# A build-time ordered attention kernel: a longer planned DMA landing, queries projected directly for the first head group, and transposes for the last four units

## The chip, the cores and the metric

The kernel runs on one core of one Trainium2 chip. The metric is the device time of one execution in microseconds (us). Every kernel was run several times; the text gives medians and the single times where they matter. A profile is of one execution. Engines are abbreviated as in the profile: PE is the matmul engine (PEld its weight loads), ACT the scalar engine, DVE the vector engine, POOL the general-purpose engine, and SP the engine that issues nearly all DMAs (SPq in the profile).

## The reference, cut to what matters

Two attention blocks are computed from their own inputs and concatenated. Block A is softmax attention over 2048 positions with 32 heads of 20 elements; block B is linear attention. Both project inputs to queries, keys and values first and project their outputs last. All inputs are bf16.

```python
# A: B, S, D, H = 1, 2048, 640, 32 ; Dh = 20
q, k, v = split(x @ wqkv)
scores = einsum("bhqd,bhkd->bhqk", q, k) * (Dh ** -0.5)
p = softmax(scores)
a = einsum("bhqk,bhkd->bhqd", p, v).reshape(B, S, D) @ wo
# B: phi(t) = where(t > 0, t + 1, exp(t)) + 1e-6 ; no softmax, num / den
...
return concatenate([a, b], axis=-1)          # (1, 2048, 1280)
```

Most of the work is in block A: 32 heads times 2048 x 2048 scores have to be exponentiated.

## The kernel before

The kernel does not leave order to the moment of execution. While it is built, a list scheduler (`_Plan`) simulates the engines with assumed durations and assumed latencies, and so fixes the order of instructions in each engine's list. On the chip each engine works through its list and waits on semaphores where data is not there. The assumed latencies therefore set no wait and no time; they only decide how much other work stands between a DMA and the instruction that uses what it brings.

```python
_LAT = {"pe": 0.16, "act": 0.12, "dve": 0.12, "pool": 0.14, "sp": 2.8, "none": 0.0}   # us

class _Plan:
    ...
    def run(self, t, s0):                    # t is the task chosen, s0 its planned start
        ...
        t.end = s0 + dur
        ...
        for k in t.kids:                     # who depends on t
            k.t0 = max(k.t0, t.end + _lat(e, k.eng))
    ...

    def spd(self, fns, deps, reads, writes, prio=2.0):      # a group of DMAs on SP
        def fn(t):
            self.sch.dma_group("sp", fns, reads=reads, writes=writes)
        return self.plan.add(_Task("sp", 0.62 * len(fns), fn, prio=prio), deps)
```

So `"sp": 2.8` says: what a DMA brings can be used 2.8 us after its issue.

Block A is cut into 8 groups of four heads and 4 columns of 512 queries: 32 "units" n, each planned to take 24.5 us. In a unit PE computes scores into banks `ps`, ACT exponentiates most of them (`f_PT<-ps`, 667 instructions in all), DVE does the rest by a polynomial (`f_Y`, `f_T`), and PE multiplies the results with the values. At the end of a unit DVE evacuates the sums (`f_OTr<-ps`) and the unit is normalised: the row sums go to a denser layout by a DMA, their reciprocals through DRAM and back as a broadcast by two more, and a multiply writes the result. The evacuation of unit n also waits for the multiply of unit n-2, because the buffer `OTr` has two halves.

```python
    def t_norm(self, n, ev):                 # ev: the evacuation of unit n
        ...
        prev = self.mult[n - 1] if n else None
        if n in self.quick:
            a = self.dve(0.62, tr1, (ev, prev), prio=0.2)    # DVE transpose  Rbc <- OTr
            a = self.dve(0.25, rc1, (a,), prio=0.2)          # reciprocal     Rc  <- Rbc
            last = self.dve(0.62, tr2, (a,), prio=0.2)       # DVE transpose  Rbc <- Rc
            pr = 0.2
        else:
            d1 = self.spd([lambda e: e.dma_start(Rc, OTr[0:128:32, o, :])],
                          (ev,), (("OTr", o),), (("Rc", o),))
            a = self.dve(0.25, rc, (d1,), prio=2.0)          # reciprocal, in place
            d2 = self.spd([lambda e: e.dma_start(nd, Rc)], (a, prev), (("Rc", o),), (("Nd", o),))
            last = self.spd([lambda e: e.dma_start(Rbc[:], nd.unsqueeze(1).broadcast_to([4, 32, 512]))],
                            (d2,), (("Nd", o),), ("Rbc",))
            pr = 2.0
        self.mult[n] = self.dve(0.62, mult, (last,) + outdep, prio=pr)    # OTw <- OTr * Rbc
        if n < self.NU - 1:
            self.ostore[n] = self.spd([...], (self.mult[n],), ...)        # Od <- OTw, 4 DMAs
```

`self.quick = {NU - 1}`: only the last unit uses the transposes. `t_oload` loads columns of `Od` back (`f_OTp<-f_Od`) for the output projection.

Queries and keys of later groups are projected for 128 channels at a time, copied to one of three `qkp` slots, stored to DRAM and loaded in the head layout (`t_qk`, `t_kload`, `t_qload`). Group 0 has its keys, and the queries of column 0, projected straight into the head layout with padded weights (`t_pad`); its queries of columns 1 to 3 take the trip through DRAM.

```python
        self.kq[("Q", 0)] = [self.t_pad("Q", 0, (ex[0],), 0.0, 0.1)]
        ...
        first = [("Q", 0, 1), ("K", 0, 0), ("K", 1, 0), ("Q", 0, 2), ...]      # 16 jobs of t_qk
        for k, (w, c2, tc) in enumerate(first):
            jobs.append((ut[1] - 9.0 + k * (ut[4] - ut[1] - 10.0) / len(first), w, c2, tc))
        ...
        self.t_qload(0, 1, 2)
        self.t_qload(0, 2, 4)
```

A mask for block B is made in five steps, each a POOL instruction and two DVE instructions that wait for each other. The plan books it as 3.0 us of POOL and no DVE.

```python
    def make_mask(self):
        for c in range(N_DC):                                  # 5 times
            sch.op("pool", lambda e: e.iota(it, ...))
            sch.op("dve", lambda e: e.tensor_scalar(mf, it, 0.0, None, op0=ALU.is_le), ...)
            sch.op("dve", lambda e: e.scalar_tensor_tensor(self.mask[:, c], it, -19.0, mf, ...), ...)
```

Of the kernel before, what the change touches and what calls it, by code (L numbers as in the profile page):

```python
# [718 lines left out]
def _lat(a, b):  # L719
    if a == b:  # L720
        return {"dve": 0.05, "sp": _LAT["sp"]}.get(a, 0.0)
    return _LAT[a]


_LAT = {"pe": 0.16, "act": 0.12, "dve": 0.12, "pool": 0.14, "sp": 2.8, "none": 0.0}


class _Task:
    __slots__ = ("eng", "dur", "fn", "left", "kids", "prio", "end", "t0", "acq", "rel", "bank",
                 "due", "win", "mode", "ready", "seq", "cond", "occ", "over", "work", "pace")  # L730

    def __init__(self, eng, dur, fn, prio=2.0, acq=None, rel=(), due=None, win=None, mode=None,
                 cond=None, occ=None, over=1.0, work=0.0, pace=False):
        self.eng = eng
        self.dur = dur
        self.occ = dur if occ is None else occ
        self.fn = fn
        self.left = 0
        self.kids = []
        self.prio = prio  # L740
        self.end = None
        self.t0 = 0.0
        self.acq = acq
        self.rel = rel
        self.bank = None
        self.due = due
        self.win = win
        self.mode = mode
        self.cond = cond
        self.over = over  # L750
        self.work = work
        self.pace = pace


class _Plan:
# [20 lines left out]
    def add(self, task, deps=()):  # L776
        task.seq = self.seq
        self.seq += 1
        self.open += 1
        for d in deps:  # L780
            if d is None:
                continue
            if d.end is None:
                d.kids.append(task)
                task.left += 1
            else:
                task.t0 = max(task.t0, d.end + _lat(d.eng, task.eng))
        if task.left == 0:
            self.avail[task.eng].append(task)
        return task  # L790
# [67 lines left out]
    def run(self, t, s0):  # L858
        e = t.eng
        self.now = s0  # L860
        self.avail[e].remove(t)
        if e == "pe" and self.filler is not None and s0 - self.free[e] > self.FGAP:
            self.filler(t, s0)
        if t.acq is not None:
            tok = self.banks[t.acq]
            x = min(tok)
            tok.remove(x)
            t.bank = x[1]
        dur, occ = t.dur, t.occ
        if e == "pe":  # L870
            if t.mode is not None and t.mode != self.mode:
                x = max(0.0, self.SW - (s0 - self.free[e]))
                dur += x
                occ += x
                self.mode = t.mode
            self.hist.append((s0, occ, t.work))
            if len(self.hist) > 64:
                del self.hist[:32]
        t.end = s0 + dur
        self.free[e] = s0 + occ  # L880
        self.busy[e] += occ
        extra = t.fn(t)
        if extra:
            t.end += extra
            self.free[e] += extra
        for pool, src in t.rel:
            b = src.bank if isinstance(src, _Task) else src
            self.banks[pool].append((t.end + _LAT[e], b))
        for k in t.kids:
            k.t0 = max(k.t0, t.end + _lat(e, k.eng))  # L890
            k.left -= 1
            if k.left == 0:
                self.avail[k.eng].append(k)
        self.open -= 1
# [20 lines left out]
class _Fast:  # L915
# [154 lines left out]
    def mid_consts(self):  # L1070
        sch, ps = self.sch, self.ps
# [4 lines left out]
               writes=("Vc0",))  # L1076
        sch.op("pool", lambda e: e.memset(vv[:, :, 21:22], 0.0), writes=("Vc1",))
        sch.op("pool", lambda e: e.memset(self.cst[:], 0.0), writes=tuple(("cst", g) for g in range(N_GRP)))
        sch.op("pool", lambda e: e.memset(self.Qr[:, 0, 512:], 0.0), writes=("Qz",))
        sch.op("pool", lambda e: e.memset(self.Qr[:, 1, :], 0.0), writes=("Qz",))  # L1080
        sch.op("pool", lambda e: e.memset(self.ones[:], 1.0), writes=("ones",))
        sch.op("pool", lambda e: e.memset(self.kvZ[:], 0.0), writes=("kvZ0",))
# [97 lines left out]
    def dve(self, dur, fn, deps, prio=2.0, rel=(), due=None):  # L1180
        return self.plan.add(_Task("dve", dur, fn, prio=prio, rel=rel, due=due), deps)

    def spd(self, fns, deps, reads, writes, prio=2.0):
        def fn(t):
            self.sch.dma_group("sp", fns, reads=reads, writes=writes)
        return self.plan.add(_Task("sp", 0.62 * len(fns), fn, prio=prio), deps)

    def t_pad(self, which, tc, deps, due, prio):
        sch, ps = self.sch, self.ps
# [2 lines left out]
        def mms(b):  # L1192
            for c in range(N_DC):
# [1 line left out]
                       start=(c == 0), stop=(c == N_DC - 1), reads=(("wpad", k), ("xT", c, tc)),  # L1195
                       writes=(("ps", b),), inc=(c == N_DC - 1))
                yield
        first, last = self.bg(mms, [512] * 5, deps, due, 1e9, prio=prio, over=1.0)
        self.use(("xT", tc), last)
        if which == "Q":  # L1200
            dst, res = self.Qr[:, 0, 0:512], (("Q", 0, 0),)
        else:
            dst, res = self.KT[:, 0, 512 * tc:512 * (tc + 1)], (("K", 0, tc),)

# [248 lines left out]
    def t_norm(self, n, ev):  # L1453
# [45 lines left out]
        if n < self.NU - 1:  # L1499
            self.ostore[n] = self.spd([lambda e, i=i: e.dma_start(  # L1500
                self.Od.ap()[80 * g + 20 * i:80 * g + 20 * i + 20, 512 * qc:512 * (qc + 1)],
                self.OTw[32 * i + 1:32 * i + 21, ow, :]) for i in range(4)], (self.mult[n],), (("OTw", ow),),
                (("Od", g, qc),))
        return self.mult[n]

    def t_oload(self, qc, part):
# [8 lines left out]
        else:  # L1515
            fns = [lambda e: e.dma_start(self.OTp[:, k, 0:4, :], od[0:512, col].rearrange("(c p) q -> p c q", p=128)),
                   lambda e: e.dma_start(self.OTp[0:48, k, 4, :], od[512:560, col])]
        return self.spd(fns, deps, rd, (("OTp", k),))

    def t_out(self, qc, tl, h, part, deps, due, prio=4.0):  # L1520
        sch, ps = self.sch, self.ps
# [43 lines left out]
            self.parts1[(tl, h)] = ev  # L1565
        if part != 1 and h == 1:
            d = self.spd([lambda e: e.dma_start(self.out[128 * t:128 * (t + 1), 0:D_MODEL], self.stage[:, s, :])],
                         (ev,), (("stage", s, 0), ("stage", s, 1)), (("out", t),))
            self.stg[(s, 0)] = self.stg[(s, 1)] = d
        return last  # L1570

# [330 lines left out]
    def run(self):  # L1902
# [10 lines left out]
        self.phil = {}  # L1913
        self.mult = {}
        self.outA = {}
        self.quick = {NU - 1}
        self.dkall = set(_LK[:max(self.m)])
        plan.banks["aux"] = [(0.0, 6), (0.0, 7)]
        plan.avail["dq"] = []
# [22 lines left out]
        self.ostore = {}  # L1942
        self.parts1 = {}
        self.xlast = []
        self.kq[("Q", 0)] = [self.t_pad("Q", 0, (ex[0],), 0.0, 0.1)]
        for tc in range(NQC):
            self.kq[("K", 0, tc)] = [self.t_pad("K", tc, (ex[tc],), ut[0] + tc * U / 4 - 4 if tc else 0.0,
                                                0.2 if tc == 0 else 2.2)]
        mid = _Task("pool", 1.0, lambda t: self.mid_consts())
        plan.add(mid, (self.kq[("Q", 0)][0],))  # L1950
        wol = plan.add(_Task("pool", 4.5, lambda t: self.wo_load()),
                       [self.kq[("K", 0, tc)][0] for tc in range(NQC)])
        for t in range(NT):
            self.t_v(t, 0, (ewv, ex[t // 4], mid), ut[0] + t * U / 16 - 1.5, 16.0)
        cons = {}
        jobs = []
        for t in range(NT):
            jobs.append((ut[2] + t * 5 * U / 16, "V", t, 1))
        first = [("Q", 0, 1), ("K", 0, 0), ("K", 1, 0), ("Q", 0, 2), ("K", 0, 1), ("K", 1, 1), ("Q", 0, 3),
                 ("K", 0, 2), ("K", 1, 2), ("K", 0, 3), ("K", 1, 3), ("Q", 1, 0), ("Q", 1, 1), ("Q", 1, 2),  # L1960
                 ("Q", 1, 3), ("Q", 0, 0)]
        for k, (w, c2, tc) in enumerate(first):
            jobs.append((ut[1] - 9.0 + k * (ut[4] - ut[1] - 10.0) / len(first), w, c2, tc))
        for c2, a, b in ((2, 4.5, 10.5), (3, 11.0, 15.0), (4, 16.0, 22.5)):
            for k in range(8):
                jobs.append((T0 + (a + (b - a) * k / 8.0) * U, "KQ"[k % 2], c2, k // 2))
# [13 lines left out]
        if max(self.m):  # L1980
            cons[0], cons[1] = self.t_const(0, ut[0] + 0.8 * U), self.t_const(1, ut[4])
            cons[2], cons[3] = self.t_const(2, ut[7]), self.t_const(3, ut[8])
        self.t_qload(0, 1, 2)
        self.t_qload(0, 2, 4)

        self.pvcnt = [0] * NU
        self.pvn = 0
# [254 lines left out]
```

## Time and profile before

Three runs gave 864.59, 867.81 and 875.27 us. The profile is of a further execution, of 876.45 us, slower than all (its span, first to last instruction, is 874.6 us).

| span 874.6 us | us |
|---|---|
| ACT busy | 783.9 |
| ACT waits, up to 22 us | 15.2 |
| ACT waits, 22 to 76 us (units 0 and 1) | 9.4 |
| ACT waits, after 76 us | 40.7 |
| after the last exponential (the tail) | 24.0 |

The waits in this table, and in all later ones, are the idle times of 0.15 us or more in front of ACT's instructions in its timeline, added up by the time at which they end. With ACT's busy time they make 873.2 of 874.6 us. ACT is the busiest engine, so with ACT's work as it is the kernel can only become shorter by fewer of these gaps.

The page of the kernel before: busy time by engine (share of the span, instructions), and the chain of work that ended last, by engine.

```profile
PE 761.6 (87%) x10902; PEld 260.4 (30%) x10902; DVE 688.7 (79%) x1137; ACT 783.9 (90%) x723; POOL 26.8 (3%) x52
...
ACT 54%; PE 20%; DVE 14%; DMA 9%; SPq 2%; issue 1%; POOL 0%; DVEq 0%; POOLq 0%
```

ACT is 90% busy, yet makes up only 54% of the chain that ended last; DVE and DMA have 23% of it together. Work of theirs stands in ACT's way. The view of waits says which (who waits, for what: us in total, times, longest us):

```profile
ACT f_PT L1421 <- PE ps L172: 59.1, 34, 9.4
...
DVE f_Rc L1488 <- DMA f_Rc<-f_OTr: 17.6, 6, 5.6
...
DVE f_OTw L1496 <- DMA f_Rbc<-f_Nd: 14.3, 6, 5.2
```

ACT waits for scores of PE. DVE waits twelve times, 31.9 us in all, for two of the DMAs of the normalisation. How one becomes the other is to be read from the timeline of the kernel before, from 128 to 146 us (start us, duration us, engine, line, operation, output<-input, shapes, count; in brackets the idle time before it and what ended it):

```profile
130.57 0.53 SPq L1247 DMA_DIRECT2D f_KT<-f_Kd  x1
...
131.15 1.61 SPq L1258 DMA_DIRECT2D f_Qr<-f_Qd  x4
...
132.86 0.75 DVE L1449 TENSOR_SCALAR_CACHE_REDUCE f_OTr<-ps,f_c 128x512 f32<-128x512 f32 x1 [0.30 <-PE ps L172]
...
133.64 0.56 SPq L1484 DMA_DIRECT2D f_Rc<-f_OTr  x1
...
142.13 0.25 DVE L1488 RECIPROCAL f_Rc<-f_Rc 128x16 f32<-128x16 f32 x1 [4.53 <-DMA f_Rc<-f_OTr]
...
142.30 1.16 DVE L2055 TENSOR_TENSOR f_T<-f_T,f_Y 128x2048 bf16<-128x2048 bf16 x1
...
143.51 0.40 PE L172 MATMUL ps<-f_T,f_V 128*22 128x512 bf16 x4 [4.29 <-DVE f_T L2055]
...
144.50 2.52 ACT L1421 ACTIVATE f_PT<-ps 128x1536 bf16<-128x1536 f32 x2 [4.44 <-PE ps L172]
```

The 8 KB of row sums were asked for at 133.64 us, right behind a load of 512 KB of keys and four loads of queries on the same queue. They were there at 142.1 us, 8.5 us later, where the plan had assumed 2.8. DVE stood at the reciprocal for 4.53 us. The polynomial's next step (`f_T`, 142.30) stands behind it in DVE's list, and PE needs `f_T` for a multiplication with the values: PE stood 4.29 us at 143.51. ACT's next scores come behind that matmul in PE's list, so ACT waited 4.44 us. The Trainium skill, "Perfetto Trace Analysis", in its part on the tensor engine ("Tensor Engine Instruction (MATMUL, LD_WEIGHTS)"), says that "ACT/DVE/GPSIMD are strict FIFO"; this trace agrees: in those 4.53 us DVE did nothing else, though `f_T` behind the reciprocal had had its inputs since 137.2 us.

There is a second way: at 661.04 us PE stood 5.37 us in front of scores, until DVE copied scores out to `f_Y` and so emptied a bank.

That the load in front makes the DMA late is read from two cases: of the 31 DMAs of row sums in this kernel, two stand right behind keys and four query loads, and they took 8.5 and 9.5 us from issue to use; the others took 2.8 to 6.6. DVE's longest wait, 5.64 us at 660.2 us, has another origin: the evacuation had ended at 650, but SP issued the DMA only at 655.9 us, because issuing four DMAs of block B (7.49 us) and four query loads (2.06 us) came first.

The first stage has its own gaps. ACT's timeline of the kernel before, from 15 to 75 us:

```profile
39.57 6.88 ACT L1421 ACTIVATE f_PT<-ps 128x1536 bf16<-128x1536 f32 x6 [2.08 <-PE ps L172]
...
52.58 22.71 ACT L1421 ACTIVATE f_PT<-ps 128x1536 bf16<-128x1536 f32 x20 [6.13 <-PE ps L172]
```

### The profile page before, as it was taken

The page shows a single profiled execution, that of the slowest core. Times are in us where ns is not written, and L with a number is a line of the kernel's source. Part 1 is how long each engine was busy: PE and PEld are TensorE (multiplying, and loading weights), DVE is VectorE, ACT ScalarE, POOL GpSimd, SP SyncE. Part 2 cuts the span into 40 slices and gives each one's busy share as a digit, 9 for nine tenths or more (in the row PEclk, how much of TensorE's full clock was granted, in tenths as well). Part 3 has the DMA queues.
Part 4 walks back from the last instruction along what each step waited for, and adds up shares of the span by engine and source line. Part 5 has one row for each costly group of instructions (what it writes and reads, how often), then busy time and mean ns, then how long its engine had stood idle before and what let it go on. Part 6 is the DMA issues. An engine that isn't in the chain of part 4 may idle for free.

```text
span 874.6 us, 24419 instructions
## 1 busy us (share of the span) xinstructions
PE 761.6 (87%) x10902; PEld 260.4 (30%) x10902; DVE 688.7 (79%) x1137; ACT 783.9 (90%) x723; POOL 26.8 (3%) x52
## 2 busy tenths in 40 slices
PE   6989897999999999888879888898997887988996
PEld 2423232333333332333322222232222222322332
DVE  3688686898898888888869787787786996977745
ACT  3879787999999999999979999998896997999980
POOL 3200000000000000000000000000000000000000
PEclk8999888999999999999989998999898998999998
DMA  8443112002013000130162242144032031111231
GB/s 219 146 96 89 38 39 59 24 16 57 24 48 70 24 31 23 29 90 15 45 110 62 45 123 66 45 66 129 25 102 94 26 113 50 53 47 56 74 101 64
DMA packets 82619, 57.57 MB, mean 66 GB/s; under 512 B 43628, under 2 KB 74444, under 8 KB 82508
## 3 DMA queue, kind: packets, MB, share of 16 engines
q1 hardware_dynamic: 79228, 53.29, 22.3%
q10 hardware_dynamic: 3280, 2.66, 1.0%
q8 instruction: 86, 1.41, 0.7%
q14 instruction: 25, 0.20, 0.1%
HBM read 29.63 MB, written 18.57 MB: 55 GB/s over the span
## 4 chain that ended last, share of the span: by engine, by line
ACT 54%; PE 20%; DVE 14%; DMA 9%; SPq 2%; issue 1%; POOL 0%; DVEq 0%; POOLq 0%
ACT f_PT L1421 53%; PE ps L172 20%; DVE f_Y L2041 5%; DMA f_Rc<-f_OTr 4%; DVE f_T L2050 3%; DMA f_Rbc<-f_Nd 2%; ACT f_ex L1585 2%; DVE f_T L2055 1%; DMA f_xT<-in_A_x_dram 1%; SPq L1797 1%; DMA f_Nd<-f_Rc 1%; DVE f_OTr L1449 1%; DVE f_qkp L1224 1%; DMA f_Bd<-f_dc 0%; DVE f_OTw L1496 0%
## 5 line engine op out<-in xcount | busy, mean ns | idle before, releaser
L1421 ACT ACTIVATE f_PT<-ps 128x1536 bf16<-128x1536 f32 (+1 forms) x667 | 770.1, 1309 | 60.4 <-PE ps L172 59.1
L172 PE MATMUL ps<-f_Qr,f_KT 32*128 32x512 bf16 x2048 | 307.5, 396 | 63.3 <-ACT f_PT L1421 46.5
L2041 DVE TENSOR_SCALAR f_Y<-ps 128x512 bf16<-128x512 f32 x380 | 254.7, 685 | 48.7 <-PE ps L172 45.8
L172 PEld LDWEIGHTS ps<-f_Qr,f_KT 32*128 32x128 bf16 x2048 | 75.5, 91 | 308.2 <-ACT f_PT L1421 230.4
L172 PE MATMUL ps<-f_PT,f_V 128*22 128x512 bf16 x1668 | 164.3, 394 | 0.0
L2055 DVE TENSOR_TENSOR f_T<-f_T,f_Y 128x2048 bf16<-128x2048 bf16 x95 | 115.4, 1215 | 2.0 <-PE ps L172 1.7
L2050 DVE TENSOR_TENSOR f_T<-f_Y 128x2048 bf16<-128x2048 bf16 x95 | 115.3, 1214 | 2.0 <-PE ps L172 0.6
L172 PE MATMUL ps<-f_T,f_V 128*22 128x512 bf16 x760 | 73.5, 389 | 15.5 <-DVE f_T L2050 8.6
L172 PE MATMUL ps<-f_xT,f_w 128*32 128x512 bf16 x800 | 63.1, 389 | 1.2 <-DVE f_Y L2041 0.4
L172 PE MATMUL ps<-f_wB,f_xB 128*32 128x320 bf16 x1280 | 63.0, 306 | 1.2 <-DVE f_Y L2041 0.7
L172 PEld LDWEIGHTS ps<-f_PT,f_V 128*22 128x22 bf16 x1668 | 40.8, 90 | 74.4 <-issue 68.2
L172 PE MATMUL ps<-f_Y,f_V 128*22 128x512 bf16 x380 | 38.3, 387 | 4.3 <-DVE f_OTr L1449 3.7
L172 PE MATMUL ps<-f_woB,f_pk 128*32 128x320 bf16 x640 | 33.3, 315 | 5.7 <-DVE f_Y L2041 5.1
L1581 DVE TENSOR_SCALAR f_r<-ps 128x320 f32<-128x320 f32 (+1 forms) x52 | 29.2, 561 | 10.3 <-PE ps L172 10.2
L1224 DVE CAST f_qkp<-ps 128x512 bf16<-128x512 f32 x40 | 27.4, 687 | 11.5 <-PE ps L172 11.3
L172 PE MATMUL ps<-f_w,f_xT 128*32 128x160 bf16 x1280 | 35.7, 245 | 0.6 <-DVE f_V L1283 0.2
L172 PEld LDWEIGHTS ps<-f_wB,f_xB 128*32 128x32 bf16 x1280 | 27.7, 97 | 27.7 <-issue 11.3
L172 PE MATMUL ps<-f_xB,f_wB 128*32 128x512 bf16 x400 | 33.0, 409 | 0.5 <-DVE f_Y L2041 0.3
L1496 DVE TENSOR_TENSOR f_OTw<-f_OTr,f_Rbc 128x512 bf16<-128x512 f32 x32 | 22.0, 688 | 14.4 <-DMA f_Rbc<-f_Nd 14.3
L1291 POOL TENSOR_SCALAR f_V<-f_V 128x160 bf16<-128x160 bf16 x24 | 15.8, 658 | 550.2 <-DVE f_V L1283 549.2
L172 PE MATMUL ps<-f_wo,f_OTp 128*32 128x320 bf16 (+1 forms) x616 | 30.8, 313 | 1.5 <-DVE f_xT L1554 0.5
L172 PEld LDWEIGHTS ps<-f_T,f_V 128*22 128x22 bf16 x760 | 18.8, 90 | 41.9 <-issue 15.3
(91 smaller groups left out, 416.7 us busy)
## 6 DMA issues: line engine op xcount, KB each, us to landing
f_Rbc<-f_Nd SPq DMA_DIRECT2D x31, 256.0 KB
f_Bd<-f_dc SPq DMA_DIRECT2D x16, 320.0 KB
f_wB<-f_Bd SPq DMA_DIRECT2D x20, 256.0 KB
out_dram<-f_st SPq DMA_DIRECT2D x32, 160.0 KB
f_KT<-f_Kd SPq DMA_DIRECT2D x7, 512.0 KB
f_Qd<-f_qkp SPq DMA_DIRECT2D x20, 128.0 KB
f_Kd<-f_qkp SPq DMA_DIRECT2D x20, 128.0 KB
f_Od<-f_OTw SPq DMA_DIRECT2D x124, 20.0 KB
```

The lines of the kernel that those rows point to most:

```text
L172: lambda e: e.matmul(out, lhsT, rhs, start=start, stop=stop, tile_position=tp, skip_group_check=sgc),
L1224: sch.op("dve", lambda e: e.tensor_copy(self.qkp[:, s, :], ps[:, first.bank, :]), reads=(("ps", first.bank),), writes=(("qkp", s),))
L1291: sch.op("pool", lambda e: e.tensor_scalar(vt[:, rs, li, :, 1:21], self.V[:, rs, t, :, 1:21], f, None, op0=ALU.mult), reads=(("V", t, rs), ...
L1421: sch.op("act", lambda e: e.activation(self.PT[:, s0:s0 + n, :], ps[:, b0:b0 + n, :], AF.Exp, scale=scale), reads=tuple(("ps", b0 + k) for ...
L1449: sch.op("dve", lambda e: e.tensor_scalar(self.OTr[:, o, :], ps[:, self.PVB, :], cs, 0.0, op0=ALU.add, op1=ALU.max, accum_out=self.mx[:, n ...
L1496: sch.op("dve", lambda e: e.tensor_tensor(self.OTw[:, ow, :], self.OTr[:, o, :], Rbc[:], op=ALU.mult), reads=("Rbc", ("OTr", o)), writes=( ...
L1581: sch.op("dve", lambda e: e.tensor_scalar(r1, ps[:, first.bank, 0:n], 0.0, 1e-6, op0=ALU.max, op1=ALU.add), reads=(("ps", first.bank),), w ...
L1585: sch.op("act", lambda e: e.activation(ex, ps[:, first.bank, 0:n], AF.Exp), reads=(("ps", first.bank),), writes=(("ex", k),))
L1797: m2 = self.spd([lambda e, j=j: e.dma_start(bd[:, j], self.dc[j:128:4, :].unsqueeze(1).broadcast_to([32, D_HEAD, 128])) for j in range(4)] ...
L2041: sch.op("dve", lambda e: e.tensor_scalar(self.Y[:, sl, :], ps[:, d.bank, :], float(D_HEAD) ** -0.5, None, op0=ALU.mult), reads=(("ps", d. ...
L2050: sch.op("dve", lambda e: e.tensor_tensor(self.T2[:, q2:q2 + 4, :], y, y, op=ALU.mult), reads=tuple(("Y", q + i) for i in range(4)), write ...
L2055: sch.op("dve", lambda e: e.tensor_tensor(self.T3[:, q3:q3 + 4, :], self.T2[:, q2:q2 + 4, :], self.Y[:, q:q + 4, :], op=ALU.mult), reads=t ...
```

## The change

Its intent is threefold: plan DMAs with a landing near what the trace shows (8.0 us), so that other work fills the time; take the first group's queries off the DRAM trip; and normalise the last four units by two DVE transposes in place of three DMAs. The transposes can do this because a head's row sums lie in a block of 32 rows. The Trainium skill, "VectorE: DVE Perf Modes" ("The three transpose paths"), says that DVE transposes only blocks of 32 x 32; that is what this layout wants, and the trace has 0.71 us for one of 128 x 512 in f32.

```diff
-_LAT = {"pe": 0.16, ..., "sp": 2.8, "none": 0.0}
+_LAT = {"pe": 0.16, ..., "sp": 8.0, "none": 0.0}
@@ class _Task: a field lat=None; _Plan.add and _Plan.run:
-            k.t0 = max(k.t0, t.end + _lat(e, k.eng))
+            k.t0 = max(k.t0, t.end + (_lat(e, k.eng) if t.lat is None else t.lat))
@@ spd(..., lat=None) hands it on @@ three exceptions to the 8.0:
+   store of a unit to Od:      lat=3.5 if n in self.quick else None
+   load of Od in t_oload:      lat=4.0
+   store of the output:        lat=4.0
@@ def t_pad
-        first, last = self.bg(mms, [512] * 5, deps, due, 1e9, prio=prio, over=1.0)
+        first, last = self.bg(mms, [512] * 5, deps, due, 1e9, prio=prio, over=0.7)
-            dst, res = self.Qr[:, 0, 0:512], (("Q", 0, 0),)
+            dst, res = self.Qr[:, 0, 512 * tc:512 * (tc + 1)], (("Q", 0, tc),)
@@
-        self.quick = {NU - 1}
+        self.quick = set(range(NU - 4, NU))
@@
-        self.kq[("Q", 0)] = [self.t_pad("Q", 0, (ex[0],), 0.0, 0.1)]
+        for tc in range(NQC):
+            self.kq[("Q", tc)] = [self.t_pad("Q", tc, (ex[tc],), ut[tc] - 9.0 if tc else 0.0, 2.2 if tc else 0.1)]
@@
-        first = [("Q", 0, 1), ("K", 0, 0), ("K", 1, 0), ("Q", 0, 2), ...]
+        first = [(w, c2, tc) for c2 in range(2) for tc in range(NQC) for w in "KQ"]
-            jobs.append((ut[1] - 9.0 + k * (ut[4] - ut[1] - 10.0) / len(first), w, c2, tc))
+            jobs.append((ut[1] + k * (ut[4] - ut[1] - 32.0) / len(first), w, c2, tc))
@@
-        self.t_qload(0, 1, 2)
-        self.t_qload(0, 2, 4)
... (a memset of Qr that is no longer needed goes; one dependence is added)
```

Read from the order of the built kernels: 60 more matmuls of the padded projection and 60 more fillers on PE; six more transposes and three more casts on DVE (three reciprocals change their form, and their number stays 36); on SP three fewer of each of the three normalisation DMAs, and eight query loads less.

More of the change, by code (lines that the diff above doesn't have):

```diff
@@ L722, in _lat @@
     return _LAT[a]
-_LAT = {"pe": 0.16, "act": 0.12, "dve": 0.12, "pool": 0.14, "sp": 2.8, "none": 0.0}
+_LAT = {"pe": 0.16, "act": 0.12, "dve": 0.12, "pool": 0.14, "sp": 8.0, "none": 0.0}
 class _Task:
     __slots__ = ("eng", "dur", "fn", "left", "kids", "prio", "end", "t0", "acq", "rel", "bank",
-                 "due", "win", "mode", "ready", "seq", "cond", "occ", "over", "work", "pace")
+                 "due", "win", "mode", "ready", "seq", "cond", "occ", "over", "work", "pace", "lat")
     def __init__(self, eng, dur, fn, prio=2.0, acq=None, rel=(), due=None, win=None, mode=None,
-                 cond=None, occ=None, over=1.0, work=0.0, pace=False):
+                 cond=None, occ=None, over=1.0, work=0.0, pace=False, lat=None):
         self.eng = eng
@@ L752, in __init__ @@
         self.pace = pace
+        self.lat = lat
 class _Plan:
@@ L786, in add @@
             else:
-                task.t0 = max(task.t0, d.end + _lat(d.eng, task.eng))
+                task.t0 = max(task.t0, d.end + (_lat(d.eng, task.eng) if d.lat is None else d.lat))
         if task.left == 0:
@@ L1078, in mid_consts @@
         sch.op("pool", lambda e: e.memset(self.cst[:], 0.0), writes=tuple(("cst", g) for g in range(N_GRP)))
-        sch.op("pool", lambda e: e.memset(self.Qr[:, 0, 512:], 0.0), writes=("Qz",))
         sch.op("pool", lambda e: e.memset(self.Qr[:, 1, :], 0.0), writes=("Qz",))
@@ L1181, in dve, with spd @@
         return self.plan.add(_Task("dve", dur, fn, prio=prio, rel=rel, due=due), deps)
-    def spd(self, fns, deps, reads, writes, prio=2.0):
+    def spd(self, fns, deps, reads, writes, prio=2.0, lat=None):
         def fn(t):
             self.sch.dma_group("sp", fns, reads=reads, writes=writes)
-        return self.plan.add(_Task("sp", 0.62 * len(fns), fn, prio=prio), deps)
+        return self.plan.add(_Task("sp", 0.62 * len(fns), fn, prio=prio, lat=lat), deps)
     def t_pad(self, which, tc, deps, due, prio):
@@ L1502, in t_norm @@
                 self.OTw[32 * i + 1:32 * i + 21, ow, :]) for i in range(4)], (self.mult[n],), (("OTw", ow),),
-                (("Od", g, qc),))
+                (("Od", g, qc),), lat=3.5 if n in self.quick else None)
         return self.mult[n]
@@ L1517, in t_oload @@
                    lambda e: e.dma_start(self.OTp[0:48, k, 4, :], od[512:560, col])]
-        return self.spd(fns, deps, rd, (("OTp", k),))
+        return self.spd(fns, deps, rd, (("OTp", k),), lat=4.0)
     def t_out(self, qc, tl, h, part, deps, due, prio=4.0):
@@ L1567, in t_out @@
             d = self.spd([lambda e: e.dma_start(self.out[128 * t:128 * (t + 1), 0:D_MODEL], self.stage[:, s, :])],
-                         (ev,), (("stage", s, 0), ("stage", s, 1)), (("out", t),))
+                         (ev,), (("stage", s, 0), ("stage", s, 1)), (("out", t),), lat=4.0)
             self.stg[(s, 0)] = self.stg[(s, 1)] = d
@@ L1951, in run @@
         wol = plan.add(_Task("pool", 4.5, lambda t: self.wo_load()),
-                       [self.kq[("K", 0, tc)][0] for tc in range(NQC)])
+                       [self.kq[("K", 0, tc)][0] for tc in range(NQC)] + [self.kq[("Q", tc)][0] for tc in range(NQC)])
         for t in range(NT):
@@ L1958, in run @@
             jobs.append((ut[2] + t * 5 * U / 16, "V", t, 1))
-        first = [("Q", 0, 1), ("K", 0, 0), ("K", 1, 0), ("Q", 0, 2), ("K", 0, 1), ("K", 1, 1), ("Q", 0, 3),
-                 ("K", 0, 2), ("K", 1, 2), ("K", 0, 3), ("K", 1, 3), ("Q", 1, 0), ("Q", 1, 1), ("Q", 1, 2),
-                 ("Q", 1, 3), ("Q", 0, 0)]
+        first = [(w, c2, tc) for c2 in range(2) for tc in range(NQC) for w in "KQ"]
         for k, (w, c2, tc) in enumerate(first):
-            jobs.append((ut[1] - 9.0 + k * (ut[4] - ut[1] - 10.0) / len(first), w, c2, tc))
+            jobs.append((ut[1] + k * (ut[4] - ut[1] - 32.0) / len(first), w, c2, tc))
         for c2, a, b in ((2, 4.5, 10.5), (3, 11.0, 15.0), (4, 16.0, 22.5)):
```

## The prediction

> **What bounds it now.** In the profiled run (span 874.6 us; busy table) ACT is busy 783.9 us (90%), PE 87%, DVE 79%; 53% of the chain that ended last is the exponentials (667, mean 1309 ns). ACT idles 91 us: about 17 before the first exponential, 24 after the last (850.6), about 49 in between, waiting for score matmuls (ACT timeline).
>
> Most of those 49 us follow a late DMA. Order is fixed at build time as if a landing took 2.8 us. In the DVE timeline reciprocals and multiplies wait for f_Rc (17.6 us) and f_Rbc (14.3 us; waits view); with DVE blocked no bank is freed and ACT starves: 4.5 us at 98 to 103, 6.3 at 144 to 151, 5.2 at 448, 2.7 at 524 to 552, 5.1 at 610 to 620, 6.6 at 663, 5.2 at 730: about 36 us. From issue to use f_Rc took 8.5 us at 133.6 and 9.5 at 435.5, behind KT and Qr loads in SP's queue. The Trainium skill (DMA: Bandwidth & Descriptors, "Anatomy of one DMA") gives about 2 us fixed for one DMA; these queued ones take longer. The first group costs 8.2 us (2.1 at 39.6, 6.1 at 52.6), where the mask's POOL/DVE steps and the queries' trip through DRAM meet.
>
> **What changes**, counted in the built kernels' order with the trace's durations:
> - Between a unit's evacuation and its reciprocal stand 7 to 14 us of DVE work (before 3 to 7), to its multiply 23 to 31 (before 10 to 16). That exceeds every wait seen (longest 5.6 us). I expect 30 to 36 us of ACT waits to go.
> - Queries of group 0: 60 more matmuls (about 6 us of PE), three casts of 0.69 us; two query loads and a memset go. But the longer landing holds the three qkp slots, and after 100 score matmuls, between units 0 and 1, stand about 15 us (estimate) of other PE work without a score (before: 5 and 9). I expect an ACT wait of about 10 us there, so no gain in the first group; two smaller clumps (4 us each) cost about 3 us.
> - Transposes for units 28 to 30: 1.4 us of DVE each, three DMA trips fewer; DVE is 46% busy at 825 to 850. Six of the eight last-but-one output tiles still stand after the last evacuation (before: all eight), so the tail shortens by 1 to 3 us.
> - 60 more filler matmuls, off the path.
>
> **Sum.** 876 (profiled) - 33 (DMA waits) + 3 (first stage) - 2 (tail) = about 844; other runs of before had fewer waits (864.6 to 875.3), so the new kernel should also scatter less. Predicted **842 us**, range 830 to 857. Faster by over 2%: 0.77; within 2%: 0.21; slower: 0.02.
>
> **The profile.** Right: DVE's waits for f_Rc and f_Rbc fall from 32 us to under 6; ACT waits after 150 us fall below 8 us; granted clock nearer 1; ACT busy unchanged within 3 us; one ACT wait of 8 to 12 us at 45 to 65 us; 20 to 24 us after the last exponential. Wrong: waits for f_Rc remain (then SP's issue order is at fault, not the planned landing), or ACT waits on PE reappear without DVE waiting for a DMA.
>
> **What would make it wrong.** The clump without scores may cost more than 12 us, or little. Longer planned landings may hold auxiliary banks and starve scores elsewhere. The profiled run is the slowest of before; against 864.6 the gain is smaller. PE, at 87%, may take back what the waits gave.

## The result, and the profile after

The changed kernel took 840.06 to 841.68 us in four runs, with a median of 840.87; the kernel before took 864.59 to 875.27 in four runs, with a median of 869.53. The ratio is 0.9668, with a 95% interval of 0.9605 to 0.9731. Ratios here are the mean time of one kernel's runs over that of the other's in the same rounds, so they are not quite the ratio of the medians. The changed kernel also scatters less: 0.2% against 1.2% from lowest to highest.

| us | before | after |
|---|---|---|
| span of the profiled run | 874.6 | 839.9 |
| ACT busy | 783.9 | 780.7 |
| ACT waits up to 22 | 15.2 | 15.8 |
| ACT waits 22 to 76 | 9.4 | 14.8 |
| ACT waits after 76 | 40.7 | 6.8 |
| tail | 24.0 | 21.1 |
| DVE waits for f_Rc and f_Rbc | 31.9 | 0 |
| mean granted PE clock | 0.953 | 0.979 |

The two profiles are of the kernel before in an execution slower than its runs, and of the slowest run of the kernel after; the medians fell by 28.7 us. The span fell by 34.7 us: 33.9 of waits after 76 us, 2.9 of tail and 3.2 of ACT's busy time, less 5.4 lost in the first stage and 0.6 at the start (the missing 0.7 us are waits too short for the table).

The page of the kernel after, busy time and chain:

```profile
PE 753.0 (90%) x11022; PEld 260.8 (31%) x11022; DVE 691.2 (82%) x1146; ACT 780.7 (93%) x723; POOL 27.9 (3%) x51
...
ACT 70%; PE 20%; DVE 7%; DMA 2%; SPq 1%; issue 1%; POOL 0%; DVEq 0%; POOLq 0%
```

DVE and DMA went from 23% of the chain to 9%, and ACT rose to 70%. The waits of the kernel after no longer have a line for `f_Rc` or `f_OTw` behind a DMA; ACT's own line is halved:

```profile
ACT f_PT L1421 <- PE ps L172: 31.2, 17, 10.1
```

The same unit end in the timeline of the kernel after, 133 to 149 us:

```profile
134.19 0.53 SPq L1247 DMA_DIRECT2D f_KT<-f_Kd  x1
134.76 1.62 SPq L1258 DMA_DIRECT2D f_Qr<-f_Qd  x4
...
136.47 0.74 DVE L1449 TENSOR_SCALAR_CACHE_REDUCE f_OTr<-ps,f_c 128x512 f32<-128x512 f32 x1
...
137.25 0.57 SPq L1484 DMA_DIRECT2D f_Rc<-f_OTr  x1
...
147.81 0.24 DVE L1488 RECIPROCAL f_Rc<-f_Rc 128x16 f32<-128x16 f32 x1
```

The DMA stands behind the same two loads as before. It was not made faster; the reciprocal now stands 10.6 us behind its issue, with DVE work in between, and has no bracket: it waits for nothing.

The first stage in the timeline of the kernel after, 40 to 80 us, PE and ACT:

```profile
56.36 1.03 PE L172 MATMUL ps<-f_Qr,f_KT 32*128 32x512 bf16 x6 [4.55 <-DVE f_Y L2038]
...
57.05 1.02 ACT L1421 ACTIVATE f_PT<-ps 128x1024 bf16<-128x1024 f32 x1 [4.06 <-PE ps L172]
...
59.67 0.61 PE L172 MATMUL ps<-f_Qr,f_KT 32*128 32x512 bf16 x2
...
67.31 0.39 PE L172 MATMUL ps<-f_PT,f_V 128*22 128x512 bf16 x4
...
67.76 12.99 ACT L1421 ACTIVATE f_PT<-ps 128x1536 bf16<-128x1536 f32 x11 [9.69 <-PE ps L172]
```

Two gaps of 4.06 and 9.69 us stand where the kernel before had 2.08 and 6.13. The first has the mask in front of it: DVE's mask steps run from 51.0 to 55.7 us, each waiting for POOL and POOL for it, and PE waits 4.55 us for a bank that DVE would have emptied. The second comes where PE's list has 140 other matmuls between two scores. They took PE 9.3 us, from 60.2 to 69.4 us; the longest such stretches of before, 80 and 92 matmuls, took it 3.5 and 4.9 us of work. (The prediction and the expectations give estimates of such stretches, counted in the built order: about 15 or 14.7 us for this one. They are too long: where the trace was looked at, PE took 0.5 to 0.7 of them.) ACT was not released by a score here: its next scores had been there since 60.3 us, and it waited until the matmuls at 67.31 us had read exponentials (`f_PT`) and so freed room in that buffer, which has 20 slots in the code. What stood in ACT's way is the stretch itself, which holds up multiplications with the values as well as scores.

### The profile page after: what moved, and what is told of

It reads as the page before. It is cut to its first block, busy times and chain, and to the rows that moved or that the text cites. A ratio compares the mean times of both kernels' runs of the same rounds, so it can differ in the third digit from the quotient of the medians.

```text
span 839.9 us, 24650 instructions
## 1 busy us (share of the span) xinstructions
PE 753.0 (90%) x11022; PEld 260.8 (31%) x11022; DVE 691.2 (82%) x1146; ACT 780.7 (93%) x723; POOL 27.9 (3%) x51
## 4 chain that ended last, share of the span: by engine, by line
ACT 70%; PE 20%; DVE 7%; DMA 2%; SPq 1%; issue 1%; POOL 0%; DVEq 0%; POOLq 0%
ACT f_PT L1421 68%; PE ps L172 20%; DVE f_Y L2038 2%; ACT f_ex L1585 2%; DMA f_xT<-in_A_x_dram 1%; DVE f_T L2047 1%; SPq L1033 1%; DMA out_dram<-f_st 0%; DVE f_T L2052 0%; DVE f_OTr L1449 0%; DVE f_st L1560 0%; DVE f_qkp L1224 0%; DVE f_woB L1131 0%; DVE f_st L1557 0%; DVE f_pk L1589 0%
## 5 line engine op out<-in xcount | busy, mean ns | idle before, releaser
L172 PE MATMUL ps<-f_Qr,f_KT 32*128 32x512 bf16 x2048 | 308.8, 388 | 53.4 <-ACT f_PT L1421 40.7
L172 PEld LDWEIGHTS ps<-f_Qr,f_KT 32*128 32x128 bf16 x2048 | 77.8, 91 | 297.7 <-ACT f_PT L1421 231.6
L172 PE MATMUL ps<-f_PT,f_V 128*22 128x512 bf16 x1668 | 159.8, 385 | 0.0
L1224 DVE CAST f_qkp<-ps 128x512 bf16<-128x512 f32 x40 | 27.4, 685 | 12.0 <-PE ps L172 11.7
L1291 POOL TENSOR_SCALAR f_V<-f_V 128x160 bf16<-128x160 bf16 x24 | 18.3, 761 | 493.0 <-DVE f_V L1283 492.0
L172 PE MATMUL ps<-f_zt 128*32 128x512 bf16 x388 | 33.5, 385 | 0.0
L172 PE MATMUL ps<-f_wo,f_OTp 128*32 128x320 bf16 x616 | 30.8, 313 | 1.4 <-DVE f_Y L2038 0.5
L1585 ACT ACTIVATE f_ex<-ps 128x320 f32<-128x320 f32 (+1 forms) x52 | 30.2, 580 | 1.3 <-DVE f_r L1581 1.2
L172 PE MATMUL ps<-f_xB,f_wB 128*32 128x512 bf16 x400 | 30.9, 383 | 0.1
```

What stands on the lines that cost most here:

```text
L172: lambda e: e.matmul(out, lhsT, rhs, start=start, stop=stop, tile_position=tp, skip_group_check=sgc),
L1224: sch.op("dve", lambda e: e.tensor_copy(self.qkp[:, s, :], ps[:, first.bank, :]), reads=(("ps", first.bank),), writes=(("qkp", s),))
L1291: sch.op("pool", lambda e: e.tensor_scalar(vt[:, rs, li, :, 1:21], self.V[:, rs, t, :, 1:21], f, None, op0=ALU.mult), reads=(("V", t, rs), ...
L1585: sch.op("act", lambda e: e.activation(ex, ps[:, first.bank, 0:n], AF.Exp), reads=(("ps", first.bank),), writes=(("ex", k),))
```

## The experiments

Twelve kernels ran, on three chips, each with the kernel before in the same rounds: its medians there were 873.91 us on chip 1, 872.94 on chip 2 and 873.19 on chip 3. All results were correct. Each kernel ran four times, land12 twice. The profile is of the fastest run of norm8_only, landing_undone, land5 and norm8_mask, and of the slowest of landing_only, queries_undone and land12, so its sums are somewhat low or high there. The table has the times and, from each profile, the sums of ACT's waits and the tail as defined above.

| kernel | chip | median us (range) | ratio to before, 95% | ACT waits 22–76 | ACT waits after 76 | tail | DVE waits f_Rc / f_Rbc |
|---|---|---|---|---|---|---|---|
| norm8_only | 1 | 856.0 (850.4–858.5) | 0.980 (0.976–0.984) | 8.0 | 7.0 | 36.9 | 0.7 / 4.2 |
| norm28_rest | 1 | 886.8 (879.2–891.1) | 1.014 (1.006–1.021) | 13.6 | 49.2 | 19.1 | 13.2 / 15.8 |
| landing_only | 1 | 864.4 (860.6–866.4) | 0.987 (0.983–0.992) | 18.5 | 9.5 | 38.1 | 5.3 / 3.3 |
| landing_undone | 1 | 878.8 (873.4–883.0) | 1.007 (1.002–1.012) | 15.3 | 39.8 | 16.3 | 14.1 / 16.8 |
| norm8_quick | 2 | 840.9 (835.8–844.0) | 0.963 (0.955–0.970) | 9.2 | 12.9 | 19.3 | 2.0 / 5.4 |
| quick_one | 2 | 859.6 (856.0–861.5) | 0.984 (0.977–0.991) | 15.2 | 8.0 | 39.2 | 0.2 / 0 |
| queries_undone | 2 | 850.8 (846.8–857.1) | 0.973 (0.967–0.980) | 17.1 | 15.9 | 21.2 | 4.7 / 3.5 |
| spread | 2 | 840.2 (837.1–842.3) | 0.963 (0.956–0.969) | 6.6 | 11.9 | 21.1 | 1.3 / 0 |
| after_again | 3 | 841.6 (839.0–842.5) | 0.964 (0.959–0.969) | 13.8 | 7.2 | 20.5 | 0 / 0 |
| norm8_mask | 3 | 841.2 (840.3–841.4) | 0.964 (0.960–0.969) | 7.2 | 10.6 | 22.8 | 0 / 0 |
| land5 | 3 | 850.2 (846.9–852.1) | 0.975 (0.970–0.980) | 13.9 | 9.9 | 23.9 | 6.7 / 0.8 |
| land12 | 3 | 975.8 (973.0–978.5) | 1.118 (1.110–1.126) | 11.7 | 127.9 | 35.2 | 0 / 1.5 |

The theories. A: the gain is the longer planned landing of the normalisation's three DMAs, because DVE stood in front of them. B, its rival: the gain is the direct queries, the transposes or the landing of the other DMAs. C: the transposes carry a part of the gain that the prediction put at 1 to 3 us; D, its rival: the tail comes from something else in the order.

### norm8_only: the kernel before, with the longer landing for three DMAs alone

The `lat` field is added with no other value changed, and then:

```diff
-                          (ev,), (("OTr", o),), (("Rc", o),))
+                          (ev,), (("OTr", o),), (("Rc", o),), lat=8.0)
-            d2 = self.spd([... nd, Rc ...], (a, prev), (("Rc", o),), (("Nd", o),))
+            d2 = self.spd([... nd, Rc ...], (a, prev), (("Rc", o),), (("Nd", o),), lat=8.0)
-                            (d2,), (("Nd", o),), ("Rbc",))
+                            (d2,), (("Nd", o),), ("Rbc",), lat=8.0)
```

> The kernel before, with 8.0 us planned only for the three landings of each unit's normalisation (f_Rc, f_Nd, f_Rbc); queries, transposes, all other landings as before. Theory A (the gain is DVE no longer blocked by these late landings): DVE's waits for f_Rc and f_Rbc fall from 32 us to under 6, ACT waits after 76 us of the span from about 41 us to under 9; about 836 us (832 to 842), so as fast as the changed kernel or a little faster, because the first stage keeps its 8 us of waits instead of 14. Theory B (the gain comes from the direct queries and the transposes, or from the other landings): 862 us or more.

Measured: 856.0 us; the waits after 76 us fell from 40.7 to 7.0 us. In the waits of norm8_only:

```profile
ACT f_PT L1422 <- PE ps L172: 24.5, 11, 9.1
...
DVE f_OTw L1497 <- DMA f_Rbc<-f_Nd: 4.2, 1, 4.2
```

Twelve waits of DVE for these DMAs became two (the other is 0.7 us long). Three planned numbers, and nothing else, take away 33.7 us of ACT's waits; the changed kernel takes away 33.9. (The profile is of the fastest of the four runs, against a slow one of before. The medians fell by 17.9 us although the tail grew by 12.9, which leaves 30.8.) But the time missed the range that A expected, 832 to 842 us: the tail grew from 24.0 to 36.9 us. The mechanism of A is right, and its bill had an entry that nobody had written down. The next experiments look for it.

### norm28_rest: the changed kernel, with the short landing for the same three DMAs

```diff
-                          (ev,), (("OTr", o),), (("Rc", o),))
+                          (ev,), (("OTr", o),), (("Rc", o),), lat=2.8)
... (the same for the other two)
```

> The changed kernel, with 2.8 us planned again only for the three landings of the normalisation. Theory A: DVE's waits for f_Rc and f_Rbc return (20 us or more) and the time goes to about 868 us (858 to 876). Theory B: the time stays within 4 us of the changed kernel's 840.9.

Measured: 886.8 us, as A said and slower than its range of 858 to 876. The waits of norm28_rest have both lines again:

```profile
DVE f_OTw L1496 <- DMA f_Rbc<-f_Nd: 15.8, 9, 4.1
...
DVE f_Rc L1488 <- DMA f_Rc<-f_OTr: 13.2, 3, 4.9
```

29.0 us of DVE's waits came back, and ACT's waits after 76 us rose to 49.2 us. So these three DMAs are necessary for the gain as well as sufficient for its main term; the 8.0 of all other DMAs, the direct queries and the transposes together do not replace them. Why this kernel is slower than landing_undone, which has 2.8 everywhere, is not settled; ACT also waits 8.0 us for DVE in block B here (`f_ex`), and the runs scatter by 12 us.

### landing_only: the kernel before, with the change's landing and nothing else

```diff
-_LAT = {..., "sp": 2.8, ...}
+_LAT = {..., "sp": 8.0, ...}
+   lat=4.0 for the load of Od and the store of the output
```

> The kernel before with the longer landing for all DMAs (4.0 for output loads and stores), without direct queries and without the three further transposes. In its order about 18 us of other PE work stand without a score between units 0 and 1 (before: 9). Theory A: waits later on vanish, the first stage loses about 8 to 10 us more than before's 8.2; about 845 us (840 to 852). Theory B: 860 us or more.

Measured: 864.4 us, which is on B's side of the expectation (860 or more), though not for B's reason: A's time left out the tail. The waits after 76 us fell to 9.5, as A said, but the first stage rose from 9.4 to 18.5 and the tail from 24.0 to 38.1. The longer landing by itself is thus worth 1.3% only. It costs twice, at the start, where the queries of columns 1 to 3 take their trip through DRAM, and at the end. The other two parts of the change work at just these two places.

### landing_undone: the changed kernel, with 2.8 everywhere

```diff
-_LAT = {..., "sp": 8.0, ...}
+_LAT = {..., "sp": 2.8, ...}
-   lat=3.5 / lat=4.0 / lat=4.0
```

> The changed kernel with 2.8 us planned for every DMA; direct queries and four transposed units stay. Theory A: waits for f_Rc and f_Rbc of 20 us or more, first stage 14 us of ACT waits as in the changed kernel, tail 21 us; about 868 us (860 to 876). Theory B: 848 us or less.

Measured: 878.8 us, no faster than before (860 to 876 was expected). Direct queries and transposes alone bring no time, and B falls. The tail is 7.7 us shorter than before (16.3 against 24.0), but the first stage waits 5.9 us longer (15.3 against 9.4). The waits of DVE for the two DMAs, from the view of waits of landing_undone:

```profile
DVE f_OTw L1496 <- DMA f_Rbc<-f_Nd: 16.8, 12, 5.4
...
DVE f_Rc L1488 <- DMA f_Rc<-f_OTr: 14.1, 3, 7.9
```

ACT's largest wait of the first stage, from its timeline in landing_undone, 20 to 80 us:

```profile
67.41 12.92 ACT L1421 ACTIVATE f_PT<-ps 128x1536 bf16<-128x1536 f32 x11 [10.32 <-PE ps L172]
```

This line matters for the prediction. It had said that the longer landing holds the `qkp` slots and so makes the large gap of the first stage. Here the landing is 2.8, and the gap is still there, at the same place, with the same 140 matmuls between two scores. So the longer landing did not make this gap.

### quick_one and norm8_quick: what the transposes are worth

quick_one is the changed kernel with the transposes for the last unit alone; norm8_quick is norm8_only with them for the last four.

```diff
 # quick_one, against the changed kernel
-        self.quick = set(range(NU - 4, NU))
+        self.quick = {NU - 1}
 # norm8_quick, against norm8_only
-        self.quick = {NU - 1}
+        self.quick = set(range(NU - 4, NU))
```

> The changed kernel with transposes for the last unit alone. Theory C: the tail rises from 21 to about 36 us, the first stage stays at 14 us of ACT waits; 856 us (851 to 860). As the prediction on record had it (transposes are worth 1 to 3 us): 844 us or less.

> The kernel before with 8.0 us planned for the normalisation's landings alone, and units 28 to 30 normalised by transposes too. norm8_only had 36.9 us after its last exponential, the changed kernel 21.1. Theory C (the three further transposes pay for the longer landing's long chains at the end; queries and other landings don't matter later on): the tail falls to about 21 us, nothing else moves; 840 us (835 to 844). Theory D (the tail comes from something else in the order): 850 us or more, tail over 30 us.

Measured: quick_one took 859.6 us, 18 us more than after_again and 19 more than its chip-mates spread and norm8_quick; its tail is 39.2 us where the changed kernel has 21.1. norm8_quick took 840.9 us, 15 less than norm8_only, with a tail of 19.3 instead of 36.9. C holds, and the size is far from 1 to 3 us. ("Nothing else moves" does not hold: the waits after 76 us rose from 7.0 to 12.9 us.) Unit 30 shows how. The timeline of quick_one, 785 to 859 us:

```profile
797.74 0.75 DVE L1449 TENSOR_SCALAR_CACHE_REDUCE f_OTr<-ps,f_c 128x512 f32<-128x512 f32 x1
...
822.24 0.67 DVE L1496 TENSOR_TENSOR f_OTw<-f_OTr,f_Rbc 128x512 bf16<-128x512 f32 x1
...
822.94 1.70 SPq L1500 DMA_DIRECT2D f_Od<-f_OTw  x4
...
827.73 0.38 SPq L1514 DMA_DIRECT2D f_OTp<-f_Od  x1
...
830.39 5.52 PE L172 MATMUL ps<-f_wo,f_OTp 128*32 128x320 bf16 x68 [4.60 <-DMA f_OTp<-f_Od]
```

The timeline of the kernel after, 785 to 840 us, for the same unit:

```profile
796.75 0.74 DVE L1449 TENSOR_SCALAR_CACHE_REDUCE f_OTr<-ps,f_c 128x512 f32<-128x512 f32 x1
...
797.54 0.71 DVE L1468 STREAM_TRANSPOSE f_Rbc<-f_OTr 128x512 f32<-128x512 f32 x1
...
799.83 0.67 DVE L1496 TENSOR_TENSOR f_OTw<-f_OTr,f_Rbc 128x512 bf16<-128x512 f32 x1
...
800.53 1.43 SPq L1500 DMA_DIRECT2D f_Od<-f_OTw  x4
...
806.54 0.43 SPq L1514 DMA_DIRECT2D f_OTp<-f_Od  x1
```

With three DMAs planned at 8.0 us each, the multiply of unit 30 runs 24.5 us after its evacuation; with the transposes, 3.1 us after. In the middle of the kernel that delay is harmless, since other units fill it. At the end nothing follows: the exponentials end at 819.4 us in quick_one, before that multiply, and the output projection then waits for the store and the load. DVE never waits for the DMAs of unit 30 in quick_one (its wait for `f_Rbc` is 0): the multiply is late because it was planned late. This is the missing entry of norm8_only: the longer landing makes the tail 13 to 15 us longer, and the transposes take that back. Their worth depends on the planned landing: with 2.8 (landing_undone) the tail is only 7.7 us shorter than before.

norm8_quick also shows what of the change is enough: two edits to the kernel before, without the direct queries and without a longer landing for other DMAs, give 840.9 us against 840.9 for the whole change (on another chip; the ratios to before are 0.963 and 0.967). Its first stage is better (9.2 against 14.8), its later waits worse (12.9 against 6.8).

### queries_undone: the changed kernel, with the queries through DRAM again

```diff
-        for tc in range(NQC):
-            self.kq[("Q", tc)] = [self.t_pad("Q", tc, ...)]
+        self.kq[("Q", 0)] = [self.t_pad("Q", 0, (ex[0],), 0.0, 0.1)]
... (over=1.0, the list `first` and its times, two t_qload and the memset as before the change)
```

> The changed kernel with the first group's queries through DRAM again. In its order 18 us of other PE work stand without a score between units 0 and 1, as in landing_only, whose ACT waits between 22 and 76 us were 18 us; the changed kernel has 14. So if the direct queries are worth only this: 845 us (842 to 849), tail 21 us.

Measured: 850.8 us with a scatter of 10 us, just above the expected 842 to 849 and some 9 to 10 more than the whole change, spread or norm8_quick. The profiled run is the slowest (857.1 us): in it the first stage has 17.1 us of waits (landing_only had 18.5), the later ones 15.9. So where all DMAs are planned with 8.0 us, the direct queries, with the times of the jobs that came with them, are worth about 1%. Only a small part of it is the first stage (17.1 against 14.8); the later waits are higher too (15.9 against 6.8), and why is not shown. Where the longer landing is given only to the normalisation (norm8_quick), the trip through DRAM costs nothing that shows; that kernel with the direct queries added was not run.

### land5 and land12: is 8.0 the right number?

```diff
-_LAT = {..., "sp": 8.0, ...}
+_LAT = {..., "sp": 5.0, ...}          # land5;  12.0 in land12
```

> The changed kernel planned with 5.0 us instead of 8.0. Between evacuation and reciprocal stand 4.5 to 12 us of DVE work, to the multiply 15 to 27. Theory A: only the longest landings still block the DVE (those that took 8 to 10 us from issue to use); DVE waits for f_Rc and f_Rbc 5 to 12 us; 849 us (842 to 856).

> The changed kernel planned with 12.0 us. Two landings and the DVE steps between them no longer fit in a unit of 24.5 us, the multiply falls to 44 to 50 us after its evacuation and holds up the evacuation two units later: in the order 25 runs of 4 to 10 us of PE work, much of it fillers, stand without a score. About 4 us of ACT wait each: 930 us (890 to 970). If a longer planned landing is only ever safer: 841 us or less.

> The changed kernel unaltered, as the yardstick of this chip: 841 us, scatter under 2 us, no wait of the DVE for f_Rc or f_Rbc.

Measured, on one chip: 850.2 us with 5.0, 841.6 with 8.0 (after_again, the changed kernel unaltered), 975.8 with 12.0. With landing_undone (2.8, 878.8 us on another chip) 8.0 is the best of the four values tried. The scatter of after_again was 3.5 us, where under 2 was expected. At 5.0 a few DMAs are still late (7.5 us of DVE's waits), and the tail is 3.4 us longer. At 12.0 DVE waits once for these DMAs, 1.5 us, and the kernel is 134 us slower than at 8.0. It was expected to be slower, but the cost was put at some 46 us too little. From DVE's timeline of land12, 405 to 444 us:

```profile
406.42 0.68 DVE L1496 TENSOR_TENSOR f_OTw<-f_OTr,f_Rbc 128x512 bf16<-128x512 f32 x1
...
407.14 0.75 DVE L1449 TENSOR_SCALAR_CACHE_REDUCE f_OTr<-ps,f_c 128x512 f32<-128x512 f32 x1
...
436.05 0.68 DVE L1496 TENSOR_TENSOR f_OTw<-f_OTr,f_Rbc 128x512 bf16<-128x512 f32 x1
...
436.77 0.75 DVE L1449 TENSOR_SCALAR_CACHE_REDUCE f_OTr<-ps,f_c 128x512 f32<-128x512 f32 x1
```

The next evacuation starts 0.7 us after each multiply. In land12, 25 of the 30 evacuations that have to wait for the multiply of two units earlier start no more than 4.0 us after it; in the changed kernel the smallest such distance is 15.6 us. The chain of normalisations has become the clock. The code says why: the second DMA of unit n waits for the multiply of unit n-1, then a landing, the third DMA, a landing, the multiply. With 12.0 that is at least 2 x (0.62 + 12.0) + 0.62 = 25.9 us planned per unit (an estimate from the planned durations), more than the 24.5 us of a unit; with 8.0 it is 17.9. ACT meets this as a full buffer: of its waits after 22 us in land12, 96.6 us end with a matmul that reads `f_PT` and so frees room for ACT's output, and not with a score. Measured, the multiplies of units 3 to 26 stand 28.8 us apart on average in land12 and 24.5 in the kernel after. 4.3 us in each of some 28 units make about 120, and ACT's waits after 76 us are 121 us longer.

### spread and norm8_mask: can the first stage be mended?

Both keep the change, give 8.0 to the normalisation's three DMAs alone (2.8 to the others, but for the three exceptions) and plan the mask in its five steps; spread also starts the projections of the next groups 10 us later.

```diff
-        mk = self.plan.add(_Task("pool", 3.0, fnm), (wk,))
+        mk = wk
+        for c in range(N_DC):
+            m1 = self.plan.add(_Task("pool", 0.3, lambda t, c=c: self.mask_iota(c)), (mk,))
+            mk = self.dve(0.6, lambda t, c=c: self.mask_cmp(c), (m1,), prio=2.5)
-            jobs.append((ut[1] + k * (ut[4] - ut[1] - 32.0) / len(first), w, c2, tc))
+            jobs.append((ut[1] + 10.0 + k * (ut[4] - ut[1] - 28.0) / len(first), w, c2, tc))   # spread
... (norm8_mask leaves the last line as the change has it; the mask's scratch moves to another buffer)
```

> The changed kernel with 8.0 us for the normalisation alone and 2.8 elsewhere, the first group's later K and Q projections due 10 us later, and the mask's steps planned one by one. The longest run of PE work without a score after the start is 4 us in its order instead of 15. If the 14 us of ACT waits between 22 and 76 us come from that run and from the unplanned mask: they fall to 5 us or less and the time to about 832 us (828 to 838). If a 2.8 us plan for the K and Q loads brings waits back elsewhere: 842 us or more.

> The changed kernel with 8.0 us for the normalisation alone, 2.8 elsewhere, and the mask's steps planned one by one; the projections' due times as in the changed kernel, so that the first K and Q loads from DRAM stand 25 to 35 scores ahead of their use (in spread 10 to 15, and the PE waited 3.8 us for one). The longest runs of PE work without a score are 5.0 and 4.6 us instead of 14.7. If the first stage's waits come from that run and the unplanned mask: ACT waits between 22 and 76 us 7 us or less, no PE wait for f_Qr; 834 us (830 to 839). If not: 840 us or more.

Measured: 840.2 and 841.2 us, the same as the changed kernel on this measure (ratios 0.963, 0.964 and 0.964). Both missed the expected times (832 and 834 us). The first stage nearly did what was wanted: 6.6 and 7.2 us of waits instead of 14.8, where 5 and 7 had been expected at most. But each got a new late DMA somewhere else. In the timeline of spread, 119 to 130 us:

```profile
125.66 1.03 PE L172 MATMUL ps<-f_Qr,f_KT 32*128 32x512 bf16 x4 [3.78 <-DMA f_Qr<-f_Qd]
...
126.29 2.36 ACT L1424 ACTIVATE f_PT<-ps 128x1536 bf16<-128x1536 f32 x2 [5.55 <-PE ps L172]
```

In the timeline of norm8_mask, 610 to 632 us:

```profile
625.57 0.95 DVE L1798 RECIPROCAL f_dc<-f_dc 128x128 f32<-128x128 f32 x1 [6.17 <-DMA f_dc<-f_dn]
...
628.85 1.02 ACT L1424 ACTIVATE f_PT<-ps 128x1024 bf16<-128x1024 f32 x1 [6.11 <-PE ps L172]
```

In spread a load of queries, issued at 122.5 us, is waited for by PE. In norm8_mask it is the reciprocal of block B, whose DMA was issued at 614.8 us and used 10.8 us later: the same head-of-line wait on DVE as before, at another DMA that has 2.8 us again. In the changed kernel, with 8.0 for these DMAs too, neither wait is there. A kernel with the planned mask and 8.0 for these DMAs as well was not run. From the two waits above it might save 6 to 7 us more, which is an estimate; its order, built and not run, keeps 132 of the 140 matmuls between two scores, so it may also save less. The changed kernel with 8.0 for the normalisation alone and the mask unplanned, built and not run, keeps all 140; norm8_mask has 48. So, of these versions, the stretch breaks up only where the mask is planned and the other DMAs have 2.8.

## Why the prediction was right, and where it was not

- **What bounds the kernel.** Right. ACT's busy time hardly moved (783.9 to 780.7 us; the prediction had said within 3 us, and 3.2 is just outside), and the gain is in ACT's waits.
- **The DMA waits, 30 to 36 us.** Right, and shown in both directions: 33.9 us in the profile of the changed kernel, 33.7 when the three landings alone are added (norm8_only), and all of it lost when they alone are taken out (norm28_rest). DVE's waits fell from 31.9 to 0 us (under 6 was said), ACT's waits after 150 us to 3.6 us (under 8 was said). Between evacuation and multiply the trace has 26 to 32 us; 23 to 31 of DVE work had been counted. The way from DVE to ACT, that "no bank is freed", is half of it: at 144 us PE waited for `f_T`, an operand, and not for a bank.
- **The first stage, 3 us lost.** Right in sign, too small: 5.4 us. A large gap was predicted and came (9.69 us, where 8 to 12 was said, but at 58 to 68 us, a little later than the 45 to 65 named). Its reason, that "the longer landing holds the three qkp slots", did not hold: the gap is the same with a landing of 2.8 (10.32 us in landing_undone). The landing counts only once the mask is planned: the stretch is then 48 matmuls with 2.8 for the other DMAs (norm8_mask) and 132 with 8.0 (built, not run). The prediction named the mask for the kernel before, but not as what would cost the new one 4 us.
- **The tail, 1 to 3 us shorter.** The number is right (2.9 us), but by luck: it is the difference of two large terms that the prediction did not have. The longer landing makes the tail 13 to 15 us longer; the transposes make it 18 us shorter (quick_one against the kernel after). The prediction counted three DMA trips fewer and two output tiles that no longer stand after the last evacuation, and took the lengthening of the normalisation only for the good that it does in the middle. For the change without the transposes the same reckoning gave 844 us or less (the expectation of quick_one); 859.6 were measured.
- **The scatter and the clock.** Right. The runs of after lie within 0.2% (those of after_again within 0.4%); the mean granted clock rose from 0.953 to 0.979. Over all kernels it goes with the waits: 0.944 to 0.962 in the runs of the four that wait most (before, norm28_rest, landing_undone, land12), 0.965 to 0.987 in the others. What causes what is not shown.

Open are the part of the direct queries' 9 us that lies after the first stage, the difference between norm28_rest and landing_undone, and the best version's time.

## What to carry to other kernels

Where order is fixed ahead of time, the latency assumed for a DMA is a tuning knob: read issue to use in the trace with the queue loaded, give that number to the DMAs in front of which an in-order engine stands, and check that a recurring chain of such landings still fits its period (at 12.0 it did not, and cost 134 us). Here 8.0 cost nothing in the middle, and 13 to 15 us at the end, where nothing follows; so shorten the chain at the end by other means. When two parts of a change look unequal, undo each alone: here the part that was priced at 1 to 3 us turned out to pay for 18.

## What the Trainium skill lacked or had wrong

- "DMA: Bandwidth & Descriptors" ("Anatomy of one DMA — SWDGE (gpsimd) path") gives about 2 us fixed for one DMA, on the path issued from the gpsimd engine. The page has no figure for a small DMA that is issued behind larger ones on one queue. Here, issued from SP, 8 KB behind 512 KB of keys and four query loads took 8.5 us from issue to use, and 10.8 us passed in norm8_mask for the DMA of `f_dc`, issued right behind keys as well; a plan with 5.0 us was still 9 us slower than one with 8.0.
- "Perfetto Trace Analysis" says that ACT, DVE and GPSIMD are strict FIFO, and this trace agrees; its sentence does not say what follows for a planned order: a late operand stops everything behind it on the engine, and with it the engines that need those results. Here 4.53 us of DVE in front of a reciprocal became 4.44 us of ACT, and twelve such waits of DVE, 31.9 us, went together with 33.9 us of ACT.
- "VectorE: DVE Perf Modes" ("The three transpose paths") has a time for a 128 x 128 bf16 transpose; for 128 x 512 in f32 that section has none. The trace shows 0.71 us, and two of them with the reciprocal and the multiply brought unit 30 from evacuation to multiply in 3.1 us.
